# Opening the second gated layer with 128-token tiles instead of a 256-token pass, with a new order of instructions, in a four-layer kernel on one Trainium2 core

## The chip, the cores and the metric

The kernel runs on one core of one Trainium2 chip. The metric is the device time of one execution in microseconds (us); of several executions the median is given. A core has five engines that run side by side, each with its own queue of instructions worked off in order: PE (matrix products), DVE (vector), ACT (activation functions, copies), POOL (small vector work) and SP (issues most DMAs). They wait for each other on semaphores. In the profile PEld is PE's loading of weights, which runs beside its products.

## The reference

Four layers on an activation of 2048 tokens x 512 features in bfloat16, each with a layer norm in front and a residual around it:

```
x = x + attention(layernorm(x))      # called A0 in the kernel, its norm L0
x = x + gated(layernorm(x))          # B1, its norm L1
x = x + attention(layernorm(x))      # A2, its norm L2 (same weights as A0)
x = x + gated(layernorm(x))          # B3, its norm L3 (same weights as B1)

attention:  q, k, v = x @ wqkv, in 32 heads of 16
            phi(u) = [softmax(u w_phi), softmax(-u w_phi)]     per head, 32 features
            kv = sum over tokens of phi(k)^T v,  z = sum of phi(k)
            o = (phi(q) kv) / (phi(q) z + 1e-6);  out = o @ wo
gated:      gate = relu(x @ W_gate), up = x @ W_up             F = 1376 columns
            out = (gate * up) @ W_down
```

An attention layer needs `kv` of all tokens before it can give the first output. The gated layer is token by token.

## The kernel before, in words

The 2048 tokens are 16 tiles of 128 (t = 0 to 15); everything stays in SBUF between layers. A feature axis of 512 is four blocks of 128, so most products come as groups of four that add up in PSUM. F = 1376 is ten chunks of 128 and a last chunk (number 10) of 96.

**An attention's second half, per tile.** The query products (`q`, L822 and L868) go to PSUM; ACT takes the exponential (`expq`, L827), DVE sums it per head (`Zq`, L847, 1204 ns), forms `rZq` (L851), `rho` (L852) and the normalized features (`phiq`, L855), SP transposes them by DMA (`qtr`, L858). Eight products of 68 columns (`num`, L921) go to PSUM banks 6 and 7, four to each; DVE takes the reciprocal of the denominators (`rden`, L927) and multiplies (`o`, L928), which frees the two banks. `otr` (L939) transposes the result: for tiles 0 and 1 on PE, with a copy out of PSUM by `evac` (L413), for the others by DMA. `wo` (L942) is four products of 512 columns, and DVE adds the residual (`resid`, L687). `center` (L700) then makes the normalized tile for the gated layer: DVE subtracts the mean (`L3 apply`, L703), the tile is transposed (`L3 tr`; tiles 0 and 1 on PE, L697, with an `evac` copy, the rest by DMA, L708), ACT sums the squares (`var`, L710), and two small operations make the scale (`vx` L712, `rx` L714).

**A gated layer.** `glu_up` (L947) works on a group of tiles as the moving side: 128, 256 or 512 tokens, that is, columns of a product. For a chunk `fc` there are four products for the gate (`Wg`) and four for up (`Wu`), all at L962, in two banks of a ring of four (0 to 3). ACT applies relu (L964) into one of three gate buffers; for most chunks ACT also copies `up` out of PSUM (L970) and DVE multiplies the two from SBUF (`h`, L972), else DVE multiplies from PSUM (L975). In B3 every chunk uses the ACT copy; in B1 every second one does up to tile 7, and none after. The last chunk is done the other way round, tokens as the output rows: four products of 192 columns per tile (`gu`, L988), relu and `h` per group (L992, L993) and one DMA transpose (`htr`, L995). `down` (L1011) is eleven products of 512 columns per tile, and DVE adds the residual with the scale of the norm (L1013). B3 stores each tile then (L1023).

**Order.** `emit` (L1026) creates the operations, each with its engine, and numbers them. The dependences come from that program order. The order in which an engine does its operations is not that order: it is written out in the tables `ORDER` (from L13), one per engine, as numbers in base 36. `Program.schedule` (L229) only follows them, `prepare` (L272) works out which semaphore waits are needed, and `emit_engine` (L323) writes them. Durations given to operations (such as 1450 for "table", L537) serve the sorting in `schedule` and an earlier planner; they put no wait into the code. For some 230 small operations (`op2`, L433) the table `CHOICE` (L377 to 410) names the engine.

**The transition from attention A2 to gated layer B3.** `emit` makes attention output for tiles 0 to 3 (`N`, L1078), then the query products of tiles 8 to 15, and then mixes the steps of the first gated group with the attention output of tile 4. In B1 the first group is tile 0, and the second, tile 1, is mixed with attention tile 4; in B3 the first group is tiles 0 and 1 together, 256 columns:

```python
            if last:
                mix(steps_B([0, 1], HA), steps_N([4]))
            else:
                for f in steps_B([0], HA):
                    f()
                mix(steps_B([1], HA), steps_N([4]))
```

Then come, for both, tiles 2 and 3 together (256 columns), tiles 4 to 7, 8 to 11 and 12 to 15 (512 columns).

**The start.** SP and ACT issue the loads. POOL fills constants (`ones` L527, `kvf` at L573 and `epsr` with zeros); PE runs products on `ones` as fillers ("dummy", L539) until real work is there; ACT loads its table with one small exponential ("table", L537), which reads `ones`.

Of the kernel before, what the change touches and what calls it, by code (L numbers as in the profile page):

```python
# [14 lines left out]
        "29 26 6 25 27 28 2a 2b 4t 2c 39 49 3u 4y 4e 44 5i 5n 58 5s 4j 6j 6k 67 73 72 8l 6d 84 6a 4o 83 8k 91 9x 9y 7r 96 9z c4 c5 9b c6 9g d9 da db b4 f9 f8 "  # L15
        "fm fl ay ee ef b2 eg gz gy fz h0 hx hw fy ij g5 g4 ik gb ga gg gh ii hv mk mj n4 n3 mu mt lm lq lt ne nd nn no nt r8 o5 o4 rf of op oq jv kn p0 pa pb "
        "vg pl pw pv vk q6 qg qh qr s1 ko sd sc sn xw xt sx sy t8 lg tt tj ti zn u4 ue u3 zu up uo uz wd wo wp x9 wz xa m8 ru ym yn xk z7 11o z8 yx 10k 11s zi "
        "10l 11v 10v 142 w2 12t yb 149 146 134 13p 135 13f 109 159 14z 13q 15a 15u 12a 15v 15k 14o 16x 178 177 17i 1b7 16m 18l 1aw 1c9 1db 1ad 1by 1d0 1e6 1dv "
        "1ea 1f0 1fg 1ew 1em 1gj 1fw 1gk 1fc 1gi 1jm 1hk 1hl 1hj 1kb 1fs 1ib 1ic 1kr 1l7 1g8 1ia 1j2 1j3 1gx 1ll 1lk 1j1 1m9 1ma 1nv 1k6 1ob 1mz 1my 1lj 1or "
        "1l3 1kn 1p7 1nn 1m8 1mn 1no 1mx 1pl 1pk 1ly 1q9 1nm 1o7 1nc 1qa 1pj 1qz 1qy 1on 1rq 1rp 1q8 1s4 1p3 1qx 1s3 1py 1ro 1t5 1t6 1s5 1s6 1t8 1qn 1t7 1u7 "  # L20
        "1ua 1u8 1xr 1uw 1uv 1u9 1xx 1y3 1uy 1ym 1yn 1ux 1z1 1z2 1y9 1yl 1zh 1zg 1z0 1zv 1zw 1zf 24t 1zu 24u 255 24v 24w 256 258 230 257 25u 25t 25h 25i 25k "
        "25w 25v 25j 26q 271 27d 272 22j 27n 27c 27z 27o 27y 289 28a 28l 28k 28v 28w 297 29h 296 29i 29t 29s 2be 23c 23x 2bp 2bq 24i 2cc 2cb 2c1 26f 2c0 2dj "
        "2cn 2cm 2di 2dt 2b3 2e5 2du 2e4 2ef 2eg 2er 2eq 2ft 2fu 2hu 2i5 2i6 2ih 2ig 2j2 2ir 2j3 2a7 2is 2d7 2kg 2k6 2kh 2k5 2l2 2l3 2ks 2kr 2mh 2le 2mg 2ld "
        "2fi 2hb 2ju 2m5 2qa 2pz 2qb 2n8 2ql 2qw 2qx 2qm 2sa 2r7 2sl 2sb 2r8 2ny 2sw 2sx 2t7 2sm 2pg 2t8 2um 2tj 2ti 2ul 2g8 2rz 2mv 2ua 2vw 2x5 2ak 2v0 2xg "
        "2xr 2xh 2od 2y3 2xs 2y2 2vd 2yd 2yp 2ye 2yo 2z0 2zb 2yz 2zm 2za 2zl 2gl 2wo 2zw 2zx 308 2wb 307 30z 2oq 31c 30m 322 "),
    "dve": (
        "2z 30 33 3a 3b 3e 3l 3m 3v 3k 3w 3p 2m 53 3z 5d 5x 5z 5t 5v 5u 60 5y 5w 7i 7g 7f 7h 6l 64 6m ao 74 ap 75 an am 85 7t 86 8m a0 7x 8n 7v a3 a1 a4 c7 ca "
        "c8 cb dc df b0 fa dg fn dd fo fb eh ek el ei em h1 h2 fq h4 hy hz h5 i1 il im i0 in io j2 j1 j3 j4 ix jd iz je iy j0 k6 jj k7 ku ky l1 l2 jo l3 l4 jp "
        "l6 l7 lv lw ju kc ly lz nu kh rc rg ki rh og ld ri o6 le or p1 rk pc pm rl vn vo q7 m5 px vq qi m6 xp qs kp s2 vs so se r4 sz xy xz t9 rr tk tu y1 u5 "
        "uf uq zr 13s we lh v0 zw zx zy zz rs vc 13t vz x0 wq w0 y8 y9 xb yo xl 13v 106 107 17w yy 15x zj 15y m9 z9 17x 15z 10m 17y 1b9 1ba 19o 10w 12u 11y 181 "  # L30
        "19p 14c 120 121 136 118 14d 13g 16c 14e 16d 150 19r 1cb 127 11k 13r 15b w3 128 1cc 18b 18c 15w 15l 1cd 14l 14m 16y 16j 16k 17j 179 17v 18i 18j 1a3 1a4 "
        "1bo 1bp 19b 1cq 1cr 18z 1aa 1ab 1b8 1dl 1ax 1dm 19n 1bv 1cx 1bw 1cy 1ca 1e8 1ds 1dt 1e7 1eb 1dc 1ey 1fe 1f3 1fh 1d1 1en 1ex 1jk 1kp 1fu 1fx 1gl 1fj "
        "1ft 12b 1k9 1fd 1l8 1ks 1gy 1dw 1hm 1g9 1hn 1j4 1j5 1gm 1id 1ha 1go 1nt 1l5 1nw 1mb 1ie 1i1 1hp 1mc 1la 1o9 1is 1k7 1jj 1p5 1oc 1gn 1os 1op 1ko 1p8 "
        "1lm 1ln 1n0 1ig 1n1 1n2 1l4 1lo 1pm 1lz 1lp 1nd 1np 1mo 1j7 1nq 1pn 1po 1r0 1pp 1r1 1o8 1r3 1qb 1qc 1s7 1s8 1oo 1p4 1rr 1rs 1se 1sf 1pz 1qo 1t9 1tg "
        "1rf 1xp 1ta 1th 1qe 201 1xs 1sw 1xv 202 203 20f 1xu 1ty 1tl 204 20g 1y1 208 209 1yo 1um 1y7 1y6 1yp 1z3 1ya 1yq 1z4 1yc 1zi 1zj 1zl 1zx 1zy 200 1zz "
        "20a 21r 21q 21s 21p 20d 221 222 227 22u 22v 22c 23n 23o 22d 20m 22i 248 249 235 236 265 23b 20n 2et 26r 266 2gm 2eu 24f 23u 23v 273 2ev 27e 2gn 280 "
        "28b 27p 2at 24g 2au 28m 2go 2lg 298 2cx 29j 28x 29u 2cy 2j5 26c 2j6 26d 2n9 2na 2f8 2f9 2bf 23d 2a6 2lh 2br 2aj 2li 2ll 2b0 2h1 2cd 2c2 2h2 2d4 2ff "
        "2co 23y 2b1 2or 2os 2dk 2nc 2d5 2fg 2e6 2eh 2dv 2es 2tl 2fv 2jk 2jl 2g7 2ra 2ou 2b4 2hv 2rb 2i7 2ow 2lv 2tm 2lw 2gk 2it 2h8 2h9 2ii 2j4 2no 2m2 2k7 "
        "2np 2rf 2m3 2jr 2js 2l4 2ki 2kt 2p6 2p7 2lf 2mi 2mu 2rp 2nv 2nw 2rq 2n7 2m6 2u0 2u1 2qc 2q0 2hc 2jv 2op 2oc 2vm 2pd 2qn 2qy 2pe 2r9 2sc 2rw 2rx 2vn "
        "2t9 2sn 2sy 2tk 2un 2uz 2u7 2u8 2vt 2vu 2vc 2x6 2xt 2ub 2xi 2wa 2yf 2wn 2y4 2yq 2s0 2zn 2z1 2zy 2zc 309 30l 30y 31b 31o 320 "),  # L40
# [375 lines left out]
class Kernel:  # L416
# [609 lines left out]
    def emit(self):  # L1026
# [45 lines left out]
        for li in (0, 2):  # L1072
# [52 lines left out]
            else:  # L1125
                for f in steps_B([0], HA):
                    f()
# [86 lines left out]
```

The softmax here doesn't subtract the row's maximum and nothing guards it: scores larger than these inputs give would overflow.

## Time and profile before

| quantity | value |
|---|---|
| median of 8 runs | 379.64 us (379.38 to 380.27) |
| profiled execution: device time | 379.19 us |
| profiled execution: span of the profile | 377.2 us |
| mean granted TensorE clock | 0.999 |
| L962 products by shape | 512 columns, 256 columns (tiles 0-1 of B3, tiles 2-3 of both), 128 columns (tiles 0 and 1 of B1) |
| busy in 236 to 248 us (of 12) | PE 11.59, DVE 10.00, ACT 8.01, POOL 0.62 |
| busy in 248 to 268 us (of 20) | PE 19.84, DVE 18.16, ACT 12.58, POOL 6.09 |
| busy in 268 to 285 us (of 17) | PE 16.89, DVE 13.38, ACT 7.82, POOL 3.97 |
| first `wo` of A2 starts | 240.13 us |
| `down` of B3 starts, tiles 0 and 1 | 259.46 and 264.06 us |

How to read it: the profile is one execution, taken by the hardware profiler; its span starts with the first instruction and is some 2 us shorter than the device time of the same execution (379.19 - 377.2). Busy times of successive matrix products overlap, as a product is still draining when the next one starts. In lines of groups, "out<-in" names the buffers, then come the tile (partitions x elements), the number of instructions, and behind a bar the busy time, the mean of one in ns, and the idle time of the engine before them with the instruction that ended it. In a timeline a line gives start, duration, engine, line of code, operation and, in brackets, the idle time before it and its releaser. "PE ps L962" is a product at line 962 that writes the buffer `ps` (PSUM).

### The profile page before, as it was taken

The page shows a single profiled execution, that of the slowest core. Times are in us where ns is not written, and L with a number is a line of the kernel's source. Part 1 is how long each engine was busy: PE and PEld are TensorE (multiplying, and loading weights), DVE is VectorE, ACT ScalarE, POOL GpSimd, SP SyncE. Part 2 cuts the span into 40 slices and gives each one's busy share as a digit, 9 for nine tenths or more (in the row PEclk, how much of TensorE's full clock was granted, in tenths as well). Part 3 has the DMA queues.
Part 4 walks back from the last instruction along what each step waited for, and adds up shares of the span by engine and source line. Part 5 has one row for each costly group of instructions (what it writes and reads, how often), then busy time and mean ns, then how long its engine had stood idle before and what let it go on. Part 6 is the DMA issues. An engine that isn't in the chain of part 4 may idle for free.

```text
span 377.2 us, 6882 instructions
## 1 busy us (share of the span) xinstructions
PE 367.2 (97%) x2519; PEld 203.4 (54%) x2565; DVE 276.2 (73%) x607; ACT 227.0 (60%) x463; POOL 130.8 (35%) x234
## 2 busy tenths in 40 slices
PE   6999999999999999999999999999999999999997
PEld 4554555877744454454444446577664454445443
DVE  5999998989968666559899999898984654342323
ACT  3999878765744127874677568584635451653450
POOL 7799941132344001350463577023221201000020
PEclk9999999999999999999999999999999999999999
DMA  7642893313326444310300045335543342142012
GB/s 239 168 82 48 197 248 132 75 33 57 78 43 98 97 60 83 70 30 14 70 2 1 3 82 94 79 63 99 79 84 83 73 91 50 28 71 70 30 42 70
DMA packets 87856, 29.33 MB, mean 78 GB/s; under 512 B 79792, under 2 KB 86800, under 8 KB 87824
## 3 DMA queue, kind: packets, MB, share of 16 engines
q1 hardware_dynamic: 84368, 25.86, 33.8%
q10 hardware_dynamic: 3456, 3.05, 2.5%
q8 instruction: 20, 0.33, 0.4%
q14 instruction: 12, 0.10, 0.1%
HBM read 7.91 MB, written 2.10 MB: 27 GB/s over the span
## 4 chain that ended last, share of the span: by engine, by line
PE 84%; POOL 7%; DVE 3%; issue 2%; ACT 1%; DMA 1%; SPq 0%; POOLq 0%; DVEq 0%
PE ps L962 37%; PE ps L1011 20%; PE ps L725 7%; PE ps L942 7%; POOL expk L750 5%; PE ps L822 5%; PE ps L988 3%; PE ps L921 2%; DMA x_sb<-in_A_x_dram 1%; PE ps L787 1%; PE ps L886 1%; DVE Zk L744 1%; POOL rstd L648 1%; PE ps L868 1%; DVE expk L755 0%
## 5 line engine op out<-in xcount | busy, mean ns | idle before, releaser
L962 PE MATMUL ps<-yT,Wgu 128*128 128x512 bf16 (+2 forms) x870 | 150.8, 320 | 0.6
L962 PEld LDWEIGHTS ps<-yT,Wgu 128*128 128x128 bf16 x880 | 78.5, 98 | 58.8 <-ACT expk L970 1.0
L964 ACT ACTIVATE gate_sb<-ps 128x512 bf16<-128x512 f32 (+2 forms) x110 | 50.7, 480 | 55.1 <-PE ps L962 40.8
L1011 PE MATMUL ps<-Wd,hT 128*128 128x512 bf16 (+4 forms) x354 | 79.3, 373 | 0.5
L1011 PEld LDWEIGHTS ps<-Wd,hT 128*128 128x128 bf16 (+1 forms) x363 | 34.7, 98 | 39.4 <-DVE hT L972 0.7
L972 DVE TENSOR_TENSOR hT<-gate_sb,expk 128x512 bf16<-128x512 bf16 (+2 forms) x70 | 23.9, 360 | 30.4 <-ACT expk L970 21.4
L970 ACT ACTIVATE expk<-ps 128x512 bf16<-128x512 f32 (+2 forms) x70 | 32.0, 475 | 22.3 <-PE ps L962 19.6
L710 ACT ACTIVATE sq<-x_sb,nmr 128x512 bf16<-128x512 bf16 x48 | 34.6, 721 | 10.3 <-DVE x_sb L687 6.6
L744 DVE TENSOR_REDUCE Zk<-expk 128x64 f32<-128x1024 bf16 x32 | 38.1, 1204 | 0.9 <-ACT expk L737 0.7
L714 POOL TENSOR_TENSOR rstd<-rv,mone 128x1 f32<-128x1 f32 x32 | 18.6, 589 | 50.3 <-DVE rv L712 50.0
L1013 DVE SCALAR_TENSOR_TENSOR x_sb<-ps,rstd,x_sb 128x512 bf16<-128x512 f32 (+2 forms) x33 | 23.9, 728 | 16.2 <-PE ps L1011 13.5
L942 PE MATMUL ps<-wo_p,oT 128*128 128x512 bf16 x118 | 30.8, 379 | 0.6 <-DVE oT L413 0.3
L975 DVE TENSOR_TENSOR hT<-gate_sb,ps 128x512 bf16<-128x512 bf16 (+2 forms) x40 | 21.7, 544 | 12.7 <-ACT gate_sb L964 6.4
L855 POOL TENSOR_TENSOR expq<-expq,rho 128x256 bf16<-128x256 bf16 x36 | 22.2, 624 | 24.4 <-DVE rho L852 23.6
L847 DVE TENSOR_REDUCE Zq<-expq 128x64 f32<-128x1024 bf16 x24 | 28.8, 1204 | 0.8 <-POOL rho L852 0.5
L687 DVE SCALAR_TENSOR_TENSOR x_sb<-ps,x_sb 128x512 bf16<-128x512 f32 x32 | 21.9, 687 | 8.7 <-PE ps L942 7.8
L750 POOL TENSOR_TENSOR expk<-expk,rZk 128x1024 bf16<-128x1024 bf16 x13 | 25.9, 2007 | 0.6 <-DVE rZk L746 0.6
L755 POOL TENSOR_TENSOR expk<-expk,rZk 128x512 bf16<-128x512 bf16 x17 | 19.1, 1134 | 11.8 <-DVE rZk L746 11.5
L822 PE MATMUL ps<-Wqp,yT 128*128 128x512 bf16 x91 | 22.8, 379 | 0.3
L725 PE MATMUL ps<-Wkp,yT 128*128 128x512 bf16 x84 | 22.0, 379 | 0.2
L725 PE MATMUL ps<-wv_p,yT 128*128 128x512 bf16 x85 | 22.0, 379 | 0.2
L712 POOL TENSOR_SCALAR rv<-rv 128x1 f32<-128x1 f32 x22 | 4.3, 204 | 45.3 <-ACT sq L710 45.3
(126 smaller groups left out, 512.7 us busy)
## 6 DMA issues: line engine op xcount, KB each, us to landing
out_dram<-x_sb ACTq DMA_DIRECT2D x15, 128.0 KB, 1.7
x_sb<-in_A_x_dram SPq DMA_DIRECT2D x3, 512.0 KB, 5.3
Wgu<-in_B_W_up_dram SPq DMA_DIRECT2D x4, 344.0 KB, 5.4
Wgu<-in_B_W_gate_dram SPq DMA_DIRECT2D x4, 344.0 KB, 4.1
Wd<-in_B_W_down_dram SPq DMA_DIRECT2D x5, 256.0 KB, 3.2
yT<-ytile SPq DMA_TRANSPOSE x56, 2.5
qT<-expq SPq DMA_TRANSPOSE x40, 2.5
x_sb<-in_A_x_dram SPq DMA_DIRECT2D x4, 128.0 KB, 3.6
```

What stands on the lines that cost most here:

```text
L710: op("act", lambda e: e.activation(k.sq[:], k.x_sb[:, t, :], ACT.Square, scale=-float(D), bias=k.nmr[:, t, :], accum_out=k.rv1[:, t, :]), ...
L725: op("pe", (lambda ic, bank, W: lambda e: e.matmul(k.pb[bank][:], k.yT[:, ic, t * 128:(t + 1) * 128], W[:, ic, :], start=(ic == 0), stop=( ...
L744: op("dve", lambda e: e.tensor_reduce(k.Zk[:, zb, :], k.expk[:, t, :, :, :].rearrange("p g s (h f) -> p (g s h) f", f=16), AX.X, ALU.add), ...
L750: op("pool", lambda e: e.tensor_tensor(kv, kv, k.rZk[:, rb, :].unsqueeze(2).to_broadcast([P, 64, 16]), ALU.mult), [r("expk", t, 0), r("exp ...
L822: op("pe", (lambda ic, bank, tt: lambda e: e.matmul(k.pb[bank][:], k.yT[:, ic, tt * 128:(tt + 1) * 128], k.Wqp[:, ic, :], start=(ic == 0), ...
L847: op("dve", lambda e: e.tensor_reduce(k.Zq[:, b, :], k.expq[:, t, :, :, :].rearrange("p g s (h f) -> p (g s h) f", f=16), AX.X, ALU.add), ...
L942: op("pe", (lambda c, bank: lambda e: e.matmul(k.pb[bank][:], k.oT[:, ob, c, :], k.wo_p[:, c, :], start=(c == 0), stop=(c == NC - 1)))(c, ...
L962: op("pe", (lambda bank, W, ic, fc, Mf: lambda e: e.matmul(k.pb[bank][0:Mf, 0:n], W[:, ic, fc * 128:fc * 128 + Mf], k.yT[:, ic, c0:c0 + n] ...
L964: op("act", (lambda Mf, gb, gs: lambda e: e.activation(k.gate_sb[0:Mf, gs, 0:n], k.pb[gb][0:Mf, 0:n], ACT.Relu))(Mf, gb, gs), [self.RP[gb] ...
L970: op("act", (lambda Mf, ub, up: lambda e: e.activation(up[0:Mf, 0:n], k.pb[ub][0:Mf, 0:n], ACT.Copy))(Mf, ub, up), [self.RP[ub]], ru, 170 ...
L972: op("dve", (lambda Mf, up, gs, u: lambda e: e.tensor_tensor(k.hT[0:Mf, u, 0:n], k.gate_sb[0:Mf, gs, 0:n], up[0:Mf, 0:n], ALU.mult))(Mf, u ...
L1011: op("pe", (lambda fc, Kf, u, c0, bank, m0, m1: lambda e: e.matmul(k.pb[bank][:, m0:m1], k.hT[0:Kf, u, c0:c0 + 128], k.Wd[0:Kf, fc, m0:m1] ...
```

## The change

**What is emitted.** B3 opens like B1: tile 0 alone, then tile 1 mixed with the attention output of tile 4, then tiles 2 and 3.

```diff
-            if last:
-                mix(steps_B([0, 1], HA), steps_N([4]))
-            else:
-                for f in steps_B([0], HA):
-                    f()
-                mix(steps_B([1], HA), steps_N([4]))
+            for f in steps_B([0], HA):
+                f()
+            mix(steps_B([1], HA), steps_N([4]))
             mix(steps_B([2, 3], HA), steps_N([5, 6, 7]))
```

There are 4076 operations instead of 3963. By engine: PE 2645 (2565 before), ACT 462 (438), DVE 574 (559), POOL 223 (230), SP 172 (171). On PE 80 products of 256 columns give way to 160 of 128.

**The order.** All five tables of `ORDER` are new, as the numbers have moved, and within them operations have changed places in every stage of the kernel. PE around the opening of B3 (a name stands for its group of four products, `num` for eight or where marked for four, `Wg 0 2` is chunk 2 of the group that begins with tile 0):

```
before: q 12, num 0, q 10, q 9, otr 0, num 1, wo 0, num 2, q 11, otr 1, q 14, L3 tr 0,
        num 3, q 13, wo 1, gu 0, q 15, num 4, L3 tr 1, wo 2, gu 1, Wg 0 0, Wu 0 1, ...
after:  q 12, num 0, q 9, num 1 x4, otr 0, num 1 x4, q 10, wo 0, num 2, q 11, otr 1, q 14,
        num 3 x4, L3 tr 0, num 3 x4, q 13, wo 1, q 15, num 4 x4, Wg 0 0, gu 0, Wu 0 0,
        num 4 x4, L3 tr 1, Wu 0 1, wo 2, Wg 0 2, Wu 0 3, Wg 0 1, Wu 0 2, wo 3, Wg 0 3,
        num 5 x4, Wg 0 4, Wu 0 4, Wu 0 5, Wg 0 5, num 5 x4, Wg 0 6 ... Wu 0 9, num 6 x4,
        Wg 0 9, Wu 1 1, gu 1, Wu 1 0, down 0, num 6 x4, Wg 1 1, ...
```

DVE in the same place, after:

```
rden 0, o 0, rden 1, o 1, phiq 5 0, resid 0, rden 2, L3 apply 0, o 2, Zq 7, L3 tr 0 copy,
rden 3, o 3, rZq 7, rho 7, resid 1, L3 apply 1, Zq 8, rden 4, h 0 10, rZq 8, rho 8,
L3 tr 1 copy, resid 2, o 4, h 0 1, h 0 0, h 0 2, resid 3, h 0 3, h 0 4, L3 vx 1, rden 5,
h 0 5, o 5, h 0 6, phiq 7 0, h 0 7, h 0 8, L3 apply 3, Zq 9, rZq 9, L3 apply 2, h 1 10,
h 0 9, Zq 10, rden 6, o 6, h 1 0, ...
```

At the start of the kernel POOL and ACT begin in another order:

```
POOL before: v ones 0, ones, ident, mask8 a, eps zero, mask8 b, mask4, kvf zero, L0 rv1 0, ...
POOL after:  kvf zero, eps zero, ones, mask8 a, ident, mask8 b, agg w0, kv ones, v ones 3, ...
ACT before:  dma wk0, dma wv1, table, dma wv0, dma wv2, dma wv3, dma wk1, dma wk2, ...
ACT after:   dma wk0, table, dma wv0, dma wv1, dma wv2, dma wv3, dma wk1, dma wk2, ...
```

**The engines.** In `CHOICE` 92 small operations change engine: 46 from POOL to DVE, 39 from DVE to POOL, 5 from DVE to ACT (four copies `numcp` of A0 and the copy of `otr 0` in A2) and 2 from ACT to DVE (`numcp 3 2` and `numcp 9 1` of A0, copies of 288 and of 432 columns).

**Without effect on the instructions.** The duration of "table" is given as 250 instead of 1450, and `CHOICE` may now send an `apply` of L0 to POOL, which it does for none.

```diff
-        op("act", lambda e: e.activation(k.sq[:, 0:1], ones_c[:, 0:1], ACT.Exp), [r("ones")], [r("sq"), r("tbl")], 1450, "table")
+        op("act", lambda e: e.activation(k.sq[:, 0:1], ones_c[:, 0:1], ACT.Exp), [r("ones")], [r("sq"), r("tbl")], 250, "table")
...
-            self.op2("act" if on_act else "dve", apply, dep, dst, {"dve": 407, "act": 825}, f"{tag} apply {t}", 250.0)
+            how = CHOICE.get(f"{tag} apply {t}", "act" if on_act else "dve")
+            other = "act" if how == "dve" else "pool" if t < 9 and how == "act" else "dve" if how == "act" else "act"
+            dd = {"dve": 407, "act": 825, "pool": 2090}
+            self.op2(how, apply, dep, dst, {e: dd[e] for e in (how, other)}, f"{tag} apply {t}", 250.0)
```

## The prediction

> **What bounds the kernel now.** I read the page, then the chain of waits in order of time, PE's waits, the groups of instructions with shapes apart, and the timelines of PE, DVE, ACT and SP around the step from the second attention to the second gated layer (235 to 285 us). Page first:
>
> ```profile
> span 377.2 us, 6882 instructions
> PE 367.2 (97%) x2519; PEld 203.4 (54%) x2565; DVE 276.2 (73%) x607; ACT 227.0 (60%) x463; POOL 130.8 (35%) x234
> ```
>
> PE is busy 97% of the span, at a granted clock of 9 in every slice, so only its own work and its waits can move the end. Busy time overlaps from one product to the next; the pace is read from the chain of waits, which counts from start to start (start, length, what):
>
> ```profile
> 78.12 1.12 PE ps L962 x20
> ...
> 252.39 4.37 PE ps L962 x40
> ...
> 374.22 0.97 DVE x_sb L1013 x2
> ```
>
> Twenty 128-column products (first gated layer) take 1.12 us, 56 ns each; forty 256-column ones (second) 4.37 us, 109 ns each. The same view gives 216 ns at 512 columns (24 in 5.18 us), 82 ns at 192, 32 ns at 68. I laid PE's starts in the timeline end to end at these paces; what is left over is waiting (the first fillers' slower pace, about 0.11 us each at 1.6, included). It is 4.7 us up to 20 us, 0.25 from there to 52, 2.7 in the first attention transition (52 to 66), 0.2 up to 205, 0.5 up to 236, **0.86 in the second transition (236 to 248.5), 0.03 from there to 285**, 0.2 later. PE's list of waits names few of them, as most are short:
>
> ```profile
> PE ps L539 <- POOL ones L527: 1.6, 1, 1.6
> PE ps L678 <- DVE ytile L670: 1.4, 1, 1.4
> ...
> PE ps L942 <- DVE oT L413: 0.3, 1, 0.3
> ```
>
> The third is in the stage that is changed. PE's timeline:
>
> ```profile
> 239.23 0.39 PE L697 MATMUL ps<-ident,osb 128*128 128x128 bf16 x4
> 239.45 0.42 PE L921 MATMUL ps<-kvbd,qT 128*128 128x68 bf16 x8
> 240.13 1.04 PE L942 MATMUL ps<-wo_p,oT 128*128 128x512 bf16 x4 [0.26 <-DVE oT L413]
> 241.21 0.41 PE L921 MATMUL ps<-kvbd,qT 128*128 128x68 bf16 x8
> ```
>
> Start to start, `wo 0` (L942) begins 0.43 us late, waiting for DVE's copy of the transpose, and `num 2` (L921) 0.21 us late, waiting for `o 1`. The rest of the 0.86 is 0.13 before the last `kvacc`, 0.07 in `num 0`, and scraps. At L962 in this stage there is no wait: **the gated layer of before does not wait for its second tile**, as products of attention stand in front.
>
> **The change, part by part.** (1) *Products.* Tiles 0 and 1 lose 80 products of 256 columns and gain 160 of 128: 160 x 55.6 - 80 x 109.1 = 8.90 - 8.73 = **+0.17 us** on PE. The eight 192-column products remain. Bounds: 0, were the paces equal per column; +7.0 us, were each 128-column product to show its weight load (98 ns mean in PEld's row; 160 x 98 - 8.7). I take 0.17: the 20 above were fed by as many weight loads.
>
> [...]
>
> (2) *Evictions.* Each 256-column pass becomes two of 128:
>
> ```profile
> L964 ACT ACTIVATE gate_sb<-ps 128x256 bf16<-128x256 f32 x30 | 10.8, 381 | 7.4 <-PE ps L962 6.0 <-DVE hT L972 0.6 <-DVE rho L852 0.5
> L964 ACT ACTIVATE gate_sb<-ps 128x128 bf16<-128x128 f32 x20 | 5.2, 277 | 2.2 <-DVE hT L972 1.0 <-PE ps L962 0.6 <-PE ps L886 0.5
> L972 DVE TENSOR_TENSOR hT<-gate_sb,expk 128x256 bf16<-128x256 bf16 x25 | 7.4, 308 | 1.8 <-ACT gate_sb L964 1.1 <-ACT expk L970 0.7
> L972 DVE TENSOR_TENSOR hT<-gate_sb,expk 128x128 bf16<-128x128 bf16 x10 | 2.3, 233 | 0.3 <-ACT gate_sb L964 0.3
> ```
>
> ACT: ten chunks of 2 x (277 + 276) instead of 381 + 382 ns, +3.4 us, and a second short relu (0.28, as in the first layer at 66.6). DVE: 10 x (2 x 233 - 308) = +1.6 us, and a second short `h` (0.25). SP: one more transpose, 1.26 us. In the stretches from 248 to 268 ACT is busy 63%, so its 3.4 us lie beside PE; DVE is busy 91%, so its 1.9 us are covered only if the new order asks for `h` late enough. That cover decides this prediction.
>
> (3) *The new order in the opening.* I walked it by hand from `num 0` (237.2), with the starts of before for what is unchanged and the spacing of this trace for the rest (ACT 0.57 per `expq`, 0.71 per `var`; DVE 0.39 + 0.61 for `rden` and `o`, 0.61 for a residual, 1.13 for `Zq`, 0.15 to 0.2 for a 128-column `h`).
> - Only `q 9` (0.86) now stands between `num 0` and the next half of `num 1`, which needs bank 6 and so `o 0`. DVE:
>
> ```profile
> 237.71 0.36 DVE L927 RECIPROCAL rden<-ps 128x32 f32<-128x32 f32 x1
> 238.10 0.69 DVE L928 TENSOR_TENSOR osb<-ps,rden 128x512 bf16<-128x512 f32 x1
> ```
>
>   `o 0` ends at 238.79; PE is there at 238.37 and goes on at about 238.85: **+0.48**.
> - Then `otr 0`, half of `num 1` and `q 10` (1.0 us) cover the copy of `otr 0`, which moves to ACT (0.59 there for `otr 1`): the 0.43 before `wo 0` goes. `q 10` and `wo 0` (1.7 us) cover `o 1`: the 0.21 goes. What is late next: `Wu 0 1` writes bank 1, which `q 15` leaves only when both its `expq` are done. ACT has 14 `expq` and two copies in a row and ends them at about 247.8; PE is there at 247.6: **+0.27**.
> - `num 5` waits for `o 4`, which in DVE's queue stands behind `Zq 8`, `rden 4`, `h 0 10`, `rZq 8`, `rho 8`, a copy and a residual: 250.7 against PE at 250.9, so 0.2 to spare. `down 0` needs `h 0 9`, queued behind `Zq 9`, `rZq 9`, two applies and `h 1 10`: 256.7, against PE's tenth product at 256.65: **+0.08**.
> - Tile 1 shows no wait in the walk up to `down 1` (gate buffers, banks, SP's transposes in their new places, the added one among them).
>
> Sum: +0.48 - 0.43 - 0.21 + 0.27 + 0.08 = **+0.19 us**. Bounds: -0.6, if none of the new waits shows; +1.3, if DVE is one `Zq` (1.13 us) later than in the walk, for PE then loses what exceeds the 0.2 at `num 5` and the rest at `down 0`.
>
> (4) *Engines.* Of the 92 small operations that change engine, 46 go from POOL to DVE, 39 the other way, 5 from DVE to ACT, 2 back. In the second attention's key stage (205 to 236, DVE 94% busy from 222 to 232) DVE loses two net L755 products of about 0.83 us: at 0, as of the 0.5 us that PE waits there 0.4 belong to the odd `kveps` shape, which stays. In the first transition DVE gains a 288-wide copy (0.45) and `zm 3` (0.27 on DVE for `zm 2`) ahead of `L1 tr 0 copy`, which had 0.39 us of idle before it: **+0.2 us** on the wait of 0.4 before the first gated product; bounds 0 and +0.7.
>
> (5) *The start.* POOL clears `kvf` (1.06 us, L573) and `epsr` (0.21) before it writes `ones`, in place of a 0.64 us fill: PE's first filler and ACT's table come about 0.6 us later, and so do the weight loads that ACT issues behind the table, `wv1` now among them. Activations are loaded by SP and get the DMA sooner. BD and the copy of `comp wk 0` move forward into the 1.4 us wait above, which takes 0.6 us (that copy) out of the way of ACT's unbroken run from 11.0 us on; a later `rstd 0` (now behind two fills and tile 2's) and `wk3` work against it. I take **-0.2 us**; bounds -0.8 and +0.6.
>
> (6) Elsewhere operations trade places within PE's stream at equal work; where it has 0.03 us of wait per 20 us I cost that at 0. The tail (the last `down`, two residuals, one store) keeps its order; more stores are queued on ACT before the last, at 0.45 us per issue beside 9 us of `down`: 0.
>
> **Sum:** 0.17 + 0.19 + 0.2 - 0.2 = +0.36 us. The profiled execution took 379.19 (span 377.2 and 2.0 around it), 0.45 below the median of 379.64; so 379.55 for a like execution, and **380.0 us** for the median. A difference within 0.2% (0.76 us) is about what a measurement of this kernel can tell from no change.
>
> **Rivals.**
> - *Slower: DVE is the bound in the opening.* With 256 columns a chunk gave DVE 0.87 us of PE time per `h`; now two cost 0.44 each while `Zq` (1.13 us) stays in its queue. If DVE reaches `o 4` more than 0.2 us later than in my walk, `num 5` stops PE, and `down 0` again. For: DVE 92% busy from 240 to 256, margin 0.2 us. Against: the first gated layer opens so with 0.1 us of wait from 72 to 90. PE loses about what DVE is late beyond that; at one `Zq` (1.13) 0.9 us more, 380.9; with the same again at `down 1` 381.8.
> - *Faster: the start gains and the opening is clean.* -0.8 at the start, no new wait at `Wu 0 1` and `down 0` (0.48 - 0.43 - 0.21 = -0.16 is left of part 3), nothing lost in the first transition: 0.17 - 0.16 - 0.8 = -0.79, so 378.85; with `num 1`'s wait gone too 378.4. It decides if `k 4` does not wait for its transpose (landed at 20.5 us in before).
> - *It does not do what it says.* PE did not wait for tile 1, so opening by tiles takes away no wait; only the reordering does. Then parts (1) and (3) stay between 0 and +0.4: inside the forecast.
>
> **Numbers.** Forecast (around 380.0, 379.0 to 380.6) 0.5, a tenth of that beyond +0.2%; slower rival 0.3; faster rival 0.2, a tenth of that within 0.2%. So faster 0.18, within 0.2% 0.47, slower 0.35. Range 378.7 to 381.4, with about a tenth outside at either end.
>
> **What will show it.** [...] Wrong would be: the start off by over 0.6 us either way, or a wait of over 0.5 us in a stage that I cost at 0.

## The result, and the profile after

The changed kernel takes 381.83 us in the median of 11 executions (381.24 to 383.31), the kernel before 379.58 beside it: a ratio of 1.0059, 95% interval 1.0049 to 1.0069, so 2.25 us slower. That is above the upper end of the forecast range (381.4), and slower by more than the 0.2% that a measurement can tell. The profiled execution took 381.46 us. From its page, span and engines:

```profile
span 379.3 us, 7084 instructions
PE 367.9 (97%) x2599; PEld 204.1 (54%) x2645; DVE 275.2 (73%) x622; ACT 229.9 (61%) x487; POOL 126.1 (33%) x227
```

The span grew by 2.1 us, PE's busy time by 0.7. As before the forecast, I laid PE's starts end to end at the paces of the chain (56 ns for a product of 128 columns, 109 for 256, 216 for 512) and summed what is left over as waiting; the first column includes the time until the first filler. In us, for the changed kernel and three of the experiments below:

| PE's waits | 0 to 30 | 30 to 52 | 52 to 90 (first transition) | 90 to 236 | 236 to the end | sum | median |
|---|---|---|---|---|---|---|---|
| before | 6.53 | 0 | 2.80 | 0.54 | 1.11 | 10.98 | 379.58 |
| after | 7.90 | 0.04 | 2.57 | 0.70 | 1.65 | 12.86 | 381.83 |
| after, with the start of before (x3) | 6.76 | 0.05 | 2.69 | 0.71 | 1.66 | 11.87 | 380.16 |
| before, with the opening of after (x2) | 6.98 | 0 | 2.69 | 0.54 | 1.41 | 11.62 | 379.74 |
| after, four edits in its start (y8) | 7.25 | 0.05 | 2.57 | 0.71 | 1.67 | 12.25 | 380.61 |

The waits of after exceed those of before by 1.88, with 0.17 for the products 2.05: the last matmul starts 2.05 us later (376.63 against 374.58). **1.37 of it arises in the first 30 us, far from the step that the change is named for.** The sums of the first column move by up to 0.45 from one profile to the next (6.53, 6.76 and 6.98 are the same start).

The opening did what the walk said, with one wait more. PE's timeline of after:

```profile
240.24 0.29 PE L927 MATMUL ps<-kvbd,qT 128*128 128x68 bf16 x4 [0.41 <-DVE osb L934]
...
241.58 1.03 PE L948 MATMUL ps<-wo_p,oT 128*128 128x512 bf16 x4
242.44 0.42 PE L927 MATMUL ps<-kvbd,qT 128*128 128x68 bf16 x8
...
249.24 0.40 PE L968 MATMUL ps<-yT,Wgu 128*128 128x128 bf16 x4
...
264.21 0.49 PE L994 MATMUL ps<-Wgu,yT 128*128 128x192 bf16 x4 [0.19 <-ACT gate_sb L970]
```

Start to start, `num 1` waits 0.57 for `o 0`, `wo 0` and `num 2` no longer wait, `Wu 0 1` comes 0.27 late, and `gu 2` 0.36: it writes the bank that `relu 1 8` empties. The chain of waits has the pace of the new products (28 in 1.56 us, 56 ns each):

```profile
253.62 1.56 PE ps L968 x28
```

In the start, first DVE's timeline, then POOL's, then PE's, all of after:

```profile
10.04 0.42 DVE L416 COPY hT<-ps 128x512 bf16<-128x512 bf16 x1 [0.27 <-PE ps L588]
10.41 1.71 DVE L676 TENSOR_SCALAR ytile<-x_sb,mv,rstd 128x512 bf16<-128x512 bf16 x1
12.04 0.40 DVE L416 COPY hT<-ps 128x512 bf16<-128x512 bf16 x1
```

```profile
9.81 0.56 POOL L634 TENSOR_TENSOR rstd<-rv,mhalf 128x1 f32<-128x1 f32 x1
10.32 0.65 POOL L571 MEMSET vsb<- 128x128 bf16 x1
10.56 0.83 POOL L574 MEMSET h10t<- 128x512 bf16 x1
11.32 0.65 POOL L571 MEMSET vsb<- 128x128 bf16 x1
```

```profile
7.66 0.38 PE L684 MATMUL ps<-ident,ytile 128*128 128x128 bf16 x4 [0.90 <-DVE mv L628]
...
12.27 0.38 PE L684 MATMUL ps<-ident,ytile 128*128 128x128 bf16 x4 [0.62 <-DVE ytile L676]
...
21.72 1.04 PE L772 MATMUL ps<-Wkp,yT 128*128 128x512 bf16 x4 [0.27 <-DMA yT<-ytile]
22.69 0.28 PE L786 MATMUL ps<-epsr,ones 1*128 1x272 bf16 x1
```

`L0 apply 3` (the second DVE line) takes 1.71 us where it took 0.41 in before; it ends at 12.12, just behind the last of three fills on POOL (11.97). `L0 ytr 3` and with it ACT's unbroken run start late, SP's transposes land 1.2 us later (`L0 tr 4` at 21.68 instead of 20.48), and PE waits for that one before `A0 k 4`. Behind `k 4` stand two `kveps` products (L786), which before had done among the fillers, at 17 and 18.5 us.

### The profile page after: what moved, and what is told of

Same layout as the page of the kernel before. It is cut to its first block, busy times and chain, and to the rows that moved or that the text cites. A ratio compares the mean times of both kernels' runs of the same rounds, so it can differ in the third digit from the quotient of the medians.

```text
span 379.3 us, 7084 instructions
## 1 busy us (share of the span) xinstructions
PE 367.9 (97%) x2599; PEld 204.1 (54%) x2645; DVE 275.2 (73%) x622; ACT 229.9 (61%) x487; POOL 126.1 (33%) x227
## 4 chain that ended last, share of the span: by engine, by line
PE 91%; DVE 4%; DMA 2%; issue 1%; ACT 1%; SPq 0%
PE ps L968 37%; PE ps L1017 20%; PE ps L731 8%; PE ps L948 7%; PE ps L828 5%; PE ps L772 4%; PE ps L994 3%; PE ps L793 2%; PE ps L874 2%; PE ps L927 2%; DVE stats L626 1%; DMA x_sb<-in_A_x_dram 1%; PE ps L892 1%; DMA yT<-ytile 1%; DVE qT L814 0%
## 5 line engine op out<-in xcount | busy, mean ns | idle before, releaser
L968 PEld LDWEIGHTS ps<-yT,Wgu 128*128 128x128 bf16 x960 | 79.3, 98 | 60.0 <-ACT expk L976 2.9
L1017 PE MATMUL ps<-Wd,hT 128*128 128x512 bf16 (+3 forms) x356 | 79.3, 372 | 0.4
L970 ACT ACTIVATE gate_sb<-ps 128x512 bf16<-128x512 f32 (+2 forms) x120 | 52.5, 455 | 43.7 <-PE ps L968 32.4
L976 ACT ACTIVATE expk<-ps 128x512 bf16<-128x512 f32 (+2 forms) x80 | 34.2, 437 | 29.3 <-PE ps L968 25.4
L861 POOL TENSOR_TENSOR expq<-expq,rho 128x256 bf16<-128x256 bf16 x31 | 19.4, 637 | 31.3 <-DVE rho L858 30.1
L761 POOL TENSOR_TENSOR expk<-expk,rZk 128x512 bf16<-128x512 bf16 x19 | 21.7, 1149 | 20.2 <-DVE rZk L752 15.4
L718 POOL TENSOR_SCALAR rv<-rv 128x1 f32<-128x1 f32 x25 | 5.6, 222 | 66.8 <-ACT sq L716 66.8
```

Source lines behind the costliest of these rows:

```text
L968: op("pe", (lambda bank, W, ic, fc, Mf: lambda e: e.matmul(k.pb[bank][0:Mf, 0:n], W[:, ic, fc * 128:fc * 128 + Mf], k.yT[:, ic, c0:c0 + n] ...
L970: op("act", (lambda Mf, gb, gs: lambda e: e.activation(k.gate_sb[0:Mf, gs, 0:n], k.pb[gb][0:Mf, 0:n], ACT.Relu))(Mf, gb, gs), [self.RP[gb] ...
L976: op("act", (lambda Mf, ub, up: lambda e: e.activation(up[0:Mf, 0:n], k.pb[ub][0:Mf, 0:n], ACT.Copy))(Mf, ub, up), [self.RP[ub]], ru, 170 ...
L1017: op("pe", (lambda fc, Kf, u, c0, bank, m0, m1: lambda e: e.matmul(k.pb[bank][:, m0:m1], k.hT[0:Kf, u, c0:c0 + 128], k.Wd[0:Kf, fc, m0:m1] ...
```

## The experiments

Diffs are given in the names of the operations, as `ORDER` has only numbers. "Before" in the measured ratios is the kernel before on the same chip.

### Which stretch loses: start and opening exchanged

Each kernel takes the order and engines of one of the two up to a cut, and of the other behind it.

```diff
 x1:  -before, 0 to 26 us      +after, 0 to 27.4 us    rest: before
 x3:  -after, 0 to 27.4 us     +before, 0 to 26 us     rest: after
 x2:  -before, from 234 us on  +after, from there on   start and middle: before
 x7:  -after, from 235 us on   +before, from there on  start and middle: after
```

x1, the start of after in before.

> The kernel before, in which only the order and the engines of what runs in the first 26 us (27.4 in the changed kernel) are those of the changed kernel. Theory S (the start loses 1.4 us of the 2.25, by the waits of PE summed up to 30 us: 7.9 against 6.5): 379.6 + 1.4 = 381.0 us, and PE's first A0 v 4 about 1.4 us later than before. Rival O (the loss lies in the opening of B3; what the start loses is given back before the end): 379.6 us, no change.

Measured 382.95 us, ratio 1.0091 (1.0077 to 1.0105). Slower than either theory: besides the late start, the queues of before behind the cut meet it badly; PE waits 1.3 us ahead of `kvacc 2` at 29.25 us for POOL, and 0.4 us three times later on. So it shows that the late start isn't given back, and not its size.

x3, the start of before in after.

> The changed kernel, in which only the order and the engines of what runs in the first 26 us are those of the kernel before. Theory S: 381.8 - 1.4 = 380.4 us. Rival O: 381.8 us, no change.

Measured 380.16 us, ratio 1.0016 (1.0007 to 1.0025). **The start is worth some 1.6 us of the 2.25** (1.67 between the two medians, 1.55 when each is taken against the kernel before beside it). Rival O is out.

x2, the opening of after in before.

> The kernel before up to 234 us, and from there the changed one: the emission of B3 by tiles, its order and its engines. This is the change of its title without the rest. Theory S: the opening alone costs 0.17 us of products and 0.6 us of waits more (1.5 against 0.9 in PE's sums from 236 to 285), 379.6 + 0.8 = 380.4 us. Rival O: all of it, 381.8 us. A third case, that the opening is free and its waits are covered elsewhere: 379.6.

Measured 379.74 us, ratio 1.0007 (0.9998 to 1.0016), that is +0.3 us (-0.1 to +0.6), with 0.30 us more waits in PE's sums from 236 us on and 0.17 of products. `num 1` (0.57) and `Wu 0 1` (0.27) wait as in after; `gu 2` hardly does (0.08). The change of the title alone can't be told from no change here.

x7, the opening of before in after.

> The changed kernel up to 235 us, and from there the kernel before (tiles 0 and 1 of B3 in one pass of 256 columns). Theory S: the start's 1.4 us stay, the first attention transition gives back 0.2 and the middle costs 0.1: 379.6 + 1.3 = 380.9 us. Rival O: 379.6 us.

Measured 380.81 us, ratio 1.0042 (1.0029 to 1.0055): with the opening undone, 1.35 us of the loss remain. By this run the opening is worth 0.9 us of the 2.25, by x2 0.3. The changed kernel's own sums lie between: 0.54 more waits from 236 us on and 0.17 of products, 0.7 together, which is also what x3 has left. The start is the larger part by every one of these.

### Which edit of the start: DVE behind POOL's fills

x9 moves one operation in the kernel before. (Its first word on each line is the engine.)

```diff
 POOL: ... rv1 3, rstd 3,
-      nrx 1,
       v ones 3, v ones 2, v ones 1, h10t zero, ...
 DVE:  ... ytrcopy 1, aggr 3, apply 2,
+      nrx 1,
       BD, wtrcopy wk 1, apply 3, wtrcopy wk 2, ...
```

> The kernel before with one operation moved: nrx 1 of L0 from POOL to DVE, behind apply 2, so that on POOL four fills (v ones 3, 2, 1, h10t zero; 10.3 to 12.6 us) follow rstd 3 at once. Theory P: L0 apply 3 waits until the last fill ends, 2.3 us instead of 0.41, L0 ytrcopy 3 on ACT comes 1.2 us later, and with it the run of ACT that feeds SP's transposes: 379.5 + 1.2 = 380.7 us. Rival Q: apply 3 at 0.4 us, time unchanged at 379.5.

Measured 380.89 us, ratio 1.0045 (1.0033 to 1.0057): **one operation of 0.15 us, moved to another engine, costs 1.6 us.** DVE's and POOL's timelines of this run:

```profile
9.66 0.42 DVE L413 COPY hT<-ps 128x512 bf16<-128x512 bf16 x1
10.07 2.21 DVE L670 TENSOR_SCALAR ytile<-x_sb,mv,rstd 128x512 bf16<-128x512 bf16 x1
12.20 0.41 DVE L413 COPY hT<-ps 128x512 bf16<-128x512 bf16 x1
```

```profile
9.98 1.72 POOL L568 MEMSET vsb<- 128x128 bf16 x3
11.31 0.82 POOL L571 MEMSET h10t<- 128x512 bf16 x1
```

`apply 3` ends just behind the fourth fill in a row (12.28 against 12.13). In before it starts at 10.08, POOL's `nrx 1` at 10.13 and the first fill at 10.30:

```profile
10.08 0.41 DVE L670 TENSOR_SCALAR ytile<-x_sb,mv,rstd 128x512 bf16<-128x512 bf16 x1
```

```profile
10.13 0.40 POOL L668 TENSOR_SCALAR nrx<-rstd 128x1 f32<-128x1 f32 x1
10.30 1.89 POOL L568 MEMSET vsb<- 128x128 bf16 x3
```

Theory P holds; it had put the cost at 1.2 us.

x4 puts the spacer back into the changed kernel.

```diff
-DVE:  ... apply 2, nrx 0, nrx 1, wtrcopy wk 1, apply 3, ...
+DVE:  ... apply 2, wtrcopy wk 1, apply 3, ...
-POOL: ... rstd 2, rstd 0, rv1 3, rstd 3, v ones 1, h10t zero, v ones 2, ...
+POOL: ... rstd 2, rstd 0, nrx 0, rv1 3, rstd 3, nrx 1, v ones 1, h10t zero, v ones 2, ...
```

> The changed kernel with two tiny operations, nrx of L0 for tiles 0 and 1 (0.15 us each on DVE), back on POOL, where the second stands between rstd 3 and three fills (v ones 1, h10t zero, v ones 2). Theory P: in the changed kernel L0 apply 3 on DVE took 1.71 us instead of 0.41, because POOL went from rstd 3 straight into these fills and DVE could not get at the buffer until the last of them ended (11.97 us); the one small operation ahead of the fills let it in first in before. Then apply 3 takes 0.4 us, L0 ytr 3 comes 0.8 us earlier, ACT's unbroken run 0.7 earlier: 381.8 - 0.7 = 381.1 us. Rival Q: apply 3 was slow for another reason (DMA traffic into the buffer, the wait on rstd 3): it stays at 1.7 us, and 381.8.

Measured 382.0 us (380.86 to 385.05 in 8 executions), ratio 1.0073 (1.0048 to 1.0097). By the median neither; the trace says that the edit wasn't what I took it for. Here `wtrcopy wk 1`, ahead of `apply 3` on DVE, waits for PE until 11.27, and `apply 3` still took 1.09 us among the fills. The spread is the subject of the next part.

x6 lets the fillers and the table start early.

```diff
-POOL: kvf zero, eps zero, ones, ...
+POOL: ones, kvf zero, eps zero, ...
```

> The changed kernel with the fill of ones first on POOL, ahead of the clearing of kvf, so that PE's fillers and ACT's table start 0.6 us or more earlier. Theory S': the fillers end in waits for tiles that come when they come (1.16 us ahead of L0 ytr 1), so nothing is gained: 381.8 us. Rival F (the late fillers are the loss, as the prediction priced them): 381.8 - 0.6 = 381.2 us or less.

Measured 383.19 us (381.45 to 384.41), ratio 1.0105 (1.0085 to 1.0126). Rival F finds no support: with PE's first filler at 1.05 us instead of 2.20, even the fastest execution (381.45) is no faster than the fastest of after (381.24). That the median is higher still goes with the half clock of the next part, which its profile shows.

x8 takes four edits back at once.

```diff
 both nrx on POOL, as in x4
-POOL: rstd 1, rv1 2, rstd 2, rstd 0, rv1 3    +POOL: rstd 1, rstd 0, nrx 0, rv1 2, rstd 2, rv1 3
-DVE:  apply 0, stats 2, apply 1, aggr 2, BD, stats 3, aggr 3, ytrcopy 1, apply 2
+DVE:  apply 0, apply 1, stats 2, aggr 2, stats 3, aggr 3, ytrcopy 1, apply 2, BD
```

> The changed kernel with four edits in its start: both nrx on POOL as above; rstd 0 on POOL right behind rstd 1 instead of ahead of rv1 3; BD on DVE behind apply 2 instead of ahead of stats 3; apply 1 on DVE ahead of stats 2, which waits for a load. Theory S': these four are what the start lost, so the time is that of the changed kernel with the whole start of before, 380.2 us (-1.6). Rival: the later fillers and loads (ones behind the clearing of kvf) keep the rest, and it is only the 0.7 of the run above: 381.1 us.

Measured 382.22 us (380.95 to 384.23), ratio 1.0083 (1.0062 to 1.0103): the theory failed here. PE's queue of after has `comp wk 0`, which needs BD, ahead of `L0 ytr 2`; with BD put back PE waits 1.7 us there. An order of DVE's can't be taken back without PE's.

### The spread: half the clock for some executions

In x8's profile the stretches by time give it away (columns: busy time of PE, PEld, DVE, ACT, POOL, then the granted clock, DMA share, GB/s), and PE's timeline beside it:

```profile
9.00:10.00 1.00, 0.00 (x0) 0.00 (x0) 1.00 (x3) 0.34 (x1) 0.84 (x3) 1.00 1.03 352
10.00:11.00 1.00, 0.84 (x9) 0.85 (x10) 0.10 (x1) 0.23 (x1) 0.99 (x3) 0.61 1.08 383
11.00:12.00 1.00, 1.00 (x11) 0.96 (x10) 0.78 (x2) 0.74 (x2) 0.83 (x2) 0.50 1.10 360
12.00:13.00 1.00, 1.00 (x4) 0.30 (x2) 0.95 (x3) 0.22 (x1) 0.00 (x0) 0.50 1.52 244
13.00:14.00 1.00, 1.00 (x10) 0.64 (x9) 1.00 (x3) 0.24 (x1) 0.00 (x0) 0.68 0.94 188
```

```profile
11.81 1.91 PE L732 MATMUL ps<-wv_p,yT 128*128 128x512 bf16 x4
```

After a pause of PE (1.7 us ahead of `comp wk 0`) the clock is halved for some 3 us; the four products take 1.91 us instead of 1.03 as in after at 7.88. x6 and x7 show it as well (0.50 to 0.7 between 8 and 13 us, after pauses of 1.6 and 2.1 us). The profiles of before, after and x3 show a clock of 1.00 from there on. A long pause alone doesn't bring it: in the profile of y3 below, PE pauses for 1.7 us ahead of `L0 ytr 1`, and its 512-column products stay 216 ns apart. In the changed kernel's own executions the two slowest (382.79 and 383.31) have a mean clock of 0.996, the other nine 1.0. y1 and y2 put 17 more fillers ahead of `L0 ytr 1`.

```diff
 y1, in after
-PE: ... A0 k 1, 4 fillers, A0 k 2, 1 filler, A0 k 3, 12 fillers, A0 v 3, ...
+PE: ... 7 + 17 fillers, L0 ytr 1, ...  A0 k 1, A0 k 2, A0 k 3, A0 v 3, ...
 y2: the same, and the four edits of x8
```

> The changed kernel with 17 of PE's 70 fillers moved: out of the places ahead of A0 k 2, k 3 and v 3 (17 to 19.5 us) to ahead of L0 ytr 1, where PE idled 1.2 to 2.1 us in the profiles. Theory K: the long idle of PE near 7 us sometimes brings its clock down (three profiles of relatives show a granted clock of 0.50 to 0.7 from 8.5 to 13.5 us, with 512-column products 427 ns apart instead of 216), which costs 0.8 to 2 us in those executions and makes the times of the changed kernel spread from 381.2 to 383.3. With the gap filled by 0.95 us of products the clock stays up: all executions at 381.2 to 381.6, median 381.4. Rival L: the spread is that of the loads alone: 381.8 median, spread over 1 us as before.

Measured 381.81 us (381.23 to 381.96), ratio 1.0059 (1.0047 to 1.0072). The spread is down to 0.7, but the median isn't: the half clock can explain the slow tail of the changed kernel, not its level. By y1 alone the smaller spread could be chance, as the five executions of y3 spread as little without these fillers.

> The four edits of the start of the run before (nrx on POOL, rstd 0, BD, apply 1) and the 17 fillers moved, together, in the changed kernel. Theory K with P: without falls of the clock the edits show what they are worth; the quickest executions with them took 380.9 against 381.3 of the changed kernel: 380.3 to 380.9 us, spread under 0.7. Rival L: 382.2 us as with the edits alone, spread 3 us.

Measured 381.1 us (380.93 to 381.16), ratio 1.0042 (1.0029 to 1.0054). The edits of x8, 382.22 without the fillers, give 0.7 with them, and the spread is 0.2 instead of 3.3: this pair, the same edits without and with the fillers, ties the slow tail to how much PE does there. It doesn't tie it to one pause, as y2 still waits 1.6 us ahead of `comp wk 0`, at full pace afterwards. The gain is smaller than expected.

### The sum of the start

a2 is the changed kernel again, beside y3 and y5.

> The changed kernel once more, beside the two runs that follow, for its level and its spread. Both theories: 381.8 us. If some executions fall into the half clock near 9 us, their times reach 382.8 or more, as 2 of 11 did before.

Measured 382.43 us (381.51 to 383.99), ratio 1.0081 (1.0062 to 1.0100). Three of its six executions took 383 and more.

```diff
 y3, in after
-PE: ... v 3, k 5, k 4, kveps 1, kvacc 0, comp wq 0, kveps 0, kvacc 0, ...
+PE: ... v 3, kveps 1, kveps 0, k 5, k 4, kvacc 0, comp wq 0, kvacc 0, ...
```

> The changed kernel with two products moved: both kveps of A0 (0.22 us each from start to start) from behind A0 k 4 to ahead of k 5. Theory W (part of the start's loss is that PE waits 0.43 us for the transpose ahead of k 4 while work that the kernel before did during the fillers, the two kveps, stands behind it): the wait is filled, 381.8 - 0.43 = 381.4 us. Rival: something later is the bound (the run of ACT that feeds SP), and what PE wins here it loses at the next wait: 381.8.

Measured 381.38 us (380.99 to 381.69), ratio 1.0051 (1.0038 to 1.0064). The wait at `k 4` is gone from PE's timeline, and the median is 0.45 us below the 381.83 of after (1.05 below a2 beside it). Part of the wait comes back further on, as the rival had it: start to start, `k 7` (25.36) now waits 0.35 for ACT, and `k 12` comes only 0.31 earlier than in after (41.09 against 41.40).

```profile
20.51 0.40 PE L787 MATMUL ps<-epsr,ones 1*128 1x272 bf16 x2
20.84 1.91 PE L773 MATMUL ps<-Wkp,yT 128*128 128x512 bf16 x8
```

y5 adds to this the 17 fillers of y1, both `nrx` on POOL, `rstd 0` and `apply 1` (BD stays).

> The changed kernel with six edits in its start: both kveps ahead of k 5, 17 fillers ahead of L0 ytr 1, both nrx on POOL, rstd 0 right behind rstd 1, apply 1 ahead of stats 2; BD stays where the change put it, since PE's comp wk 0 needs it there. Theory W with P: DVE's apply 3 no longer waits for the fills, SP's transposes come 0.7 us earlier, and the kveps fill what is left of the waits at k 5 and k 4: 381.8 - 0.7 - 0.43 = 380.7 us, near the 380.2 of the run with the whole start of before, and a spread under 0.7. Rival: 381.1 us, as in the run with the edits of DVE and POOL alone, since the kveps win nothing.

Measured 381.53 us (380.92 to 381.67), ratio 1.0051 (1.0039 to 1.0063). Missed: `wtrcopy wk 1` again kept `apply 3` until 10.61, the fills began at 10.66, and it took 1.85 us. A spacer of 0.2 us on POOL is a race, and no cure. y6 takes the fills out of the place.

```diff
 y6, in after
-POOL: ... mhalf, agg w1, rv1 1, ... rstd 3, v ones 1, h10t zero, v ones 2, rv1 4, ...
+POOL: ... mhalf, agg w1, v ones 1, h10t zero, v ones 2, rv1 1, ... rstd 3, rv1 4, ...
 y7: the same, and the kveps of y3
 y8: the same as y7, and apply 1 ahead of stats 2, rstd 0 behind rstd 1
```

> The changed kernel with the three fills of POOL that follow rstd 3 (v ones 1, h10t zero, v ones 2) moved ahead of rv1 1, to about 4.3 to 6 us, where DVE's apply 0 meets them instead of apply 3. Theory P: apply 3 takes 0.4 us for certain (the two nrx on POOL were too thin a spacer: there apply 3 still took 1.1 to 1.9), ACT's run and SP's transposes come 0.7 us earlier: 381.8 - 0.7 = 381.1 us. Rival: the transposes are not what sets the end; 381.8 or more, as apply 0 pays.

Measured 382.16 us (380.76 to 383.42), ratio 1.0068 (1.0047 to 1.0089). The median is inconclusive: two executions took 380.76 and 381.13, four 382 to 383.4, and in the profiled one (381.98) four products near 9 us start 427 ns apart, though its clock column says 1.00. The trace is clear on P: `apply 3` took 0.41, and `apply 0`, which now meets the fills, 1.09 instead of 0.34.

> The run above, and both kveps ahead of k 5 as well, which alone gave 0.4 us. Theories P and W add up: 381.8 - 0.7 - 0.4 = 380.7 us. Rival: they are one and the same wait, and the second adds nothing: 381.1 us.

Measured 380.78 us (380.66 to 382.02), ratio 1.0040 (1.0027 to 1.0053). As P and W together said. DVE's timeline of this run:

```profile
4.94 1.03 DVE L673 TENSOR_SCALAR ytile<-x_sb,mv 128x512 bf16<-128x512 bf16 x1
...
10.63 0.41 DVE L677 TENSOR_SCALAR ytile<-x_sb,mv,rstd 128x512 bf16<-128x512 bf16 x1
```

> The run above with apply 1 ahead of stats 2 (which waits for a load) and rstd 0 right behind rstd 1 as well, BD unmoved. If the idle of PE ahead of L0 ytr 1 is part of the loss: 380.3 to 380.5 us, near the 380.2 with the whole start of before. If that idle only moves to comp wk 0: 380.7 us, the same as above.

Measured 380.61 us (380.44 to 380.82), ratio 1.0030 (1.0019 to 1.0040). Nearer to the second case: PE's wait at `L0 ytr 1` falls from 0.7 to 0.2, that at `comp wk 0` grows from 0.7 to 1.3. So two causes, the fills and the place of the `kveps`, make 1.05 of the start's 1.67 us (381.83 to y7); the two smaller edits add 0.2 at most, and the spread is 0.4. Some 0.4 us against x3 are left. The wait of 0.35 ahead of `k 7`, which y3, y7 and y8 have and x3 hasn't, is about as long; no run takes it away.

### Is there a better opening?

z1 reorders PE alone in the kernel before, z2 has the order of the changed kernel between 26 and 235 us as well.

```diff
-PE: num 1, wo 0, num 2, q 11, otr 1, q 14, L3 tr 0, num 3, q 13, wo 1, gu 0, q 15, num 4, ...
+PE: num 1, q 11, wo 0, num 2, otr 1, q 14, q 13, L3 tr 0, num 3, wo 1, q 15, gu 0, num 4, ...
```

> The kernel before (256-column pass), in which only PE's order at the attention transition is changed: q 11 ahead of wo 0, q 13 ahead of L3 tr 0, q 15 ahead of gu 0. Theory: the two waits there (0.43 us at wo 0 for the copy of otr 0, 0.21 at num 2 for o 1) need other products in front, not smaller tiles; with them 379.5 - 0.5 = 379.0 us. Rival: the waits move on to L3 tr 0 and gu 0, which wait for DVE: 379.5.

Measured 380.05 us, ratio 1.0016 (1.0007 to 1.0026). My theory failed; the rival has the mechanism, waits for DVE further on, but neither the places nor the price. The waits at `wo 0` and `num 2` went, and came back larger at `otr 1` (0.70) and `wo 1` (0.52), which wait for DVE:

```profile
242.84 0.40 PE L697 MATMUL ps<-ident,osb 128*128 128x128 bf16 x4 [0.54 <-DVE x_sb L687]
...
245.80 0.38 PE L942 MATMUL ps<-wo_p,oT 128*128 128x512 bf16 x1 [0.36 <-DVE yT L413]
```

> The start of the kernel before (26 us), the order and engines of the changed kernel from there to 235 us, then the kernel before with the order of the run above. Theory: the first attention transition is 0.1 to 0.2 us shorter in the changed kernel (PE's waits from 52 to 90 us: 2.57 to 2.69 against 2.8), the rest equal: 0.15 below the run above, 378.85 us. Rival: the seam or the middle gives it back: 379.0 to 379.5.

Measured 380.01 us, ratio 1.0011 (1.0002 to 1.0020); one execution, the profiled one, took 1708.5 us with all products of PE slowed (those of 512 columns 0.84 us apart instead of 0.216) and is left out of that. Nothing gained. No version that I found beats the kernel before.

## Why the prediction was wrong, step by step

- **What bounds the kernel: right.** PE is the bound, and the loss is PE's waits: 1.88 us of them and 0.17 of products make up the 2.05 by which the last matmul is later.
- **(1) Products, +0.17: right.** 56 ns each, with no wait left over between them. The mean weight load of 98 ns, the upper bound, would have shown as 7 us here.
- **(2) Evictions: right.** 278 ns for ACT's relu of 128 columns, covered; in after PE is busy 19.55 of 20 us from 248 to 268, and neither `num 5` nor `down 0` waits.
- **(3) The opening, +0.19: mechanism right, size short.** `num 1` waits 0.57 (said 0.48), `wo 0` and `num 2` don't wait, `Wu 0 1` 0.27 (said 0.27), `down 0` 0 (said 0.08). What I missed is `gu 2`, 0.36, where the walk "shows no wait", and 0.17 instead of 0.07 in `num 0`. Waits from 236 us on are 0.54 more than before, inside the bound of 1.3; alone in before, the opening measures +0.3 (x2), undone in after 0.9 (x7).
- **(4) First transition, +0.2: it didn't come.** 2.57 against 2.80 in PE's sums; but with the start of before the two orders wait alike, 2.69 (x3 and x2), so neither a loss nor a gain of the new order is shown.
- **(5) The start, -0.2 with bounds -0.8 and +0.6: this is the step that failed.** It cost 1.4 us in the profile and 1.6 in time (x3), and `A0 v 3`, PE's first product after the last filler, starts at 19.55 instead of 19.13. I priced the late fillers, the loads, BD and `rstd 0`, all on the queues where they stand. I didn't price what the two `nrx` that leave POOL do there: with them gone, fills follow `rstd 3` at once, and DVE's `apply 3`, released by the same `rstd 3`, waits for all of them (0.6 us between y3 and y7, 1.6 us in x9). And I didn't price real work moved behind a wait: the `kveps` behind `k 4` (0.45, y3). The clock, which falls near 8 to 10 us in some executions (to 0.50 in the profiles of x6, x7 and x8), goes with the slow tail.
- **(6) Elsewhere, 0:** 0.2 between 30 and 52 and from 90 to 236 us together, a tenth of the result.
- **The rivals.** DVE as the bound of the opening, at `num 5` and `down 0`, didn't come about; the slower side was right for another reason. "It does not do what it says" was right about the opening: x2 is within 0.2% of before. The condition of the faster rival, that `k 4` doesn't wait for its transpose, was the right place to look at, and it failed: `k 4` waited 0.43.

## What to carry to other kernels

When small operations change engine, look not only at what they cost where they go, but at what moves up into their place where they left, and whether it takes something that the other engine is about to need. In a stage where PE is waiting anyway, check that real work isn't put behind the last wait while fillers stand ahead of it. A change that comes with a new order everywhere is to be weighed stage by stage: here the named step cost 0.3 to 0.9 us, the start some 1.6.

## What the runs showed of the hardware

**A DVE `tensor_scalar` from buffer to buffer waited for POOL's fills, for several in a row.** 0.41 us alone, 1.71 beside three fills, 2.21 beside four (x9), and 1.03 to 1.09 instead of 0.34 for `apply 0` (y7, y6). A copy of DVE's out of PSUM beside such fills kept its 0.42 (10.41 us in before). In x9 the wait lasted through four fills, the last of which ends at 12.13 and `apply 3` at 12.28. In the profile POOL's next fill begins before the one ahead ends (10.56 against 10.97 in after); that this is why one wait covers several is not shown.

**PE's clock was halved in some executions, for about 3 us in the stretch from 8 to 14 us** (granted 0.50 at the lowest in the profiles of x6, x7 and x8), which follows a start with many gaps: 512-column products 427 ns apart instead of 216. In the profiles of x4, x6, x7 and x8 a pause of PE of 1.6 to 2.1 us stands ahead of it. The length of one pause doesn't decide it: y6 fell after 0.8 us, while 1.5 us in a2, 1.6 in y2 and 1.7 in y3 left the pace up. What decides isn't shown; with 17 more fillers ahead of `L0 ytr 1` (y1, y2, y5) none of 15 executions took over 382.0. In x4 and y6 the pace was halved while the clock column read 1.00, so the pace is the surer sign.
